# The gate by u moves into the first MLP, sums alternate between bank pairs, and weight decoding is spread over attention

## The chip, the cores and the metric

The kernel runs on one core of one Trainium2 chip. The metric is the device time in microseconds of one launch. The engines are TensorE (PE, with its weight loads as PEld), VectorE (DVE), ScalarE (ACT) and GpSimd (POOL). SyncE (SP) issues nearly all of the DMAs, in the order of the program.

## What is computed

Three stages follow one another, on 2 x 3008 = 6016 tokens of 256 features:

```python
scores = (1.0 / S) * np.matmul(z, z.transpose(0, 2, 1))     # z: 2 x 3008 x 64
x = u * np.matmul(np.maximum(scores, 0.0) ** 2, v)          # u, v: 2 x 3008 x 256
h = x @ w_in                                                # 256 x 2048
x = (s * np.maximum(h, 0.0) ** 2 + b) @ w_out               # 2048 x 256
h = x @ w_in2
out = (h / (1.0 + np.exp(-1.702 * h))) @ w_out2
```

The MLP weights come as 64-bit numbers. The kernel turns them into 32-bit ones with integer and float operations on DVE and ACT ("decoding").

## The kernel before

**Steps.** The work is a hand-written list of 288 attention steps and then 2 x 12 x 16 = 384 MLP steps. Each step has three parts: `up` (the first matmuls), `between` (what DVE and ACT do with their result) and `down` (matmuls that add into a sum). The main loop, at the end of the kernel, emits `up` and `between` four steps (`LAG`) ahead of `down`. Beside that, `when(step, f, ...)` hangs a piece of other work on a step: loads, splits, decoding. PE, DVE, ACT, POOL and the DMA queue of SP each run their instructions in the order in which this loop emits them.

**Attention.** Scores are symmetric, so each block of 512 x 512 is computed once. `Fresh` (a block of keys kc against a row of queries c) computes scores in `up`; in `between` it takes relu and square on ACT, turns the block in tiles of 32 on DVE (`turn`, when kc < c) and splits it into a high part (`hi`) and a rest (`lo`); in `down` it adds up six matmuls a step. The turned block is written to HBM (`park`, 1 MB) and read back later (`fetch`, 4 x 256 KB), and `Turned` uses it: `between` is only the split, `down` is six matmuls into a sum of its own, and at its end DVE adds that sum to x (line 384). A batch has rows c = 0 to 5, and row c has c + 1 fresh blocks of four steps each; a turned block runs between fresh ones, at least two blocks after its own. Batch 0 is steps 0 to 143, batch 1 steps 144 to 287. The last row of a batch (c = 5, 448 queries wide) is steps 96 to 143 and 240 to 287; it ends with two turned blocks in a row.

**Sums.** Each sum takes a pair of PSUM banks from `acc_pair`. `Fresh` always takes pair A, `Turned` always pair B, and the MLP alternates by token block. The next sum in a pair has to wait until the one before has been read: by the ACT copy of line 331 (a row's x) or by the DVE addition of line 384.

**The gate.** u is loaded transposed in tiles of 32 (`load_u`, line 170: four DMAs for half the features of one 512-token block, in runs of 128 bytes), turned on DVE (`turn_u`, line 182), and multiplied into x when the x of a block is complete. For c < 5 that is POOL at line 387, after the last addition; for c = 5 it is DVE at line 333, straight from the sum. The loads and turns hang on the steps around the end of each x, which lie at steps 106 to 140 and 250 to 284.

**Decoding.** `slots` gives the layer-0 weights the steps 20 to 179, one after the other, with five parts for each of 32 tiles: line 206, lines 209 and 211, line 215, line 218, line 224. The raw tile is loaded by line 193 or 195 six slots ahead, the result goes to HBM at line 227. Layer-1 weights are decoded in the same way during the first MLP. `fetch_w` (line 231) reads a decoded tile back five steps ahead of `split_w` (lines 237 and 238); for layer 0 that is steps 244 to 278.

**First MLP.** `split_x` makes a high part and a rest of x for a token block, 9 steps ahead of the block's first step (15 for block 0). A token block is 16 steps.

Of the kernel before, what the change touches and what calls it, by code (L numbers as in the profile page):

```python
# [11 lines left out]
ALU = mybir.AluOpType  # L12
# [3 lines left out]
def attention_mlp_mlp_kernel(  # L16
# [20 lines left out]
    nc = tc.nc  # L37
    B, S, D = u.shape
# [3 lines left out]
    P = 128  # L42
    CH = 512
    TPC = CH // P
# [31 lines left out]

    def mid_tile(name, dtype=F32):
        kind = name[0]
        bufs = {"z": 3, "w": 4, "u": 5}[kind]
        return mid.tile([P, CH], dtype, tag=kind, name=name, bufs=bufs)  # L80

    def acc_pair(which, name):
        return [acc_p.tile([P, CH], F32, tag=f"acc{which}", name=f"{name}{d}") for d in range(2)]

    def width(c):
        return min(CH, S - c * CH)

    zA, zB, vt, uT, xT = {}, {}, {}, {}, {}
    staged = {}

    def queries(bb, c):
# [67 lines left out]
        eng = nc.vector if (bb, c) == (0, 0) else nc.gpsimd  # L163
        eng.tensor_tensor(out=w[:, 1, :], in0=raw[:, t, :], in1=w[:, 0, :], op=ALU.subtract)  # L164

    def load_u(bb, c, h):
        n = width(c)
        ur = mid_tile(f"ur_{bb}_{c}_{h}").rearrange("p (t a) -> p t a", a=32)
        for i in range(4):
            nc.sync.dma_start(  # L170
                out=ur[32 * i : 32 * i + 32, : n // 32, :],
                in_=u[bb, c * CH : c * CH + n, h * P + 32 * i : h * P + 32 * i + 32].rearrange(
                    "(t b) a -> b t a", b=32
                ),
            )
        staged["u", bb, c, h] = ur

    def turn_u(bb, c, h):
        n = width(c)
        ur = staged.pop(("u", bb, c, h))  # L180
        uT[bb, c, h] = mid_tile(f"ut_{bb}_{c}_{h}")
        nc.vector.transpose(out=uT[bb, c, h][:, :n], in_=ur[:, : n // 32, :].rearrange("p t a -> p (t a)"))


    wi, wo = {}, {}
# [69 lines left out]
    class Fresh:  # L255
# [60 lines left out]

        def down(self):
            if (self.kc, self.t) == (0, 0):
                self.acc[:] = acc_pair("A", "acc")
            last = self.kc == self.c and self.t == TPC - 1  # L320
            add_up(
                self.acc, vt[self.bb, self.kc, self.t], self.hi, self.lo, self.n,
                (self.kc, self.t) == (0, 0), last, self.whole,
            )
            if not last:
                return
            bb, c, n = self.bb, self.c, self.n
            x = xT[bb * NCH + c] = big_tile(f"x_{bb}_{c}").rearrange("p (d n) -> p d n", d=2)
            for d in range(2):
                if c < LASTC:  # L330
                    nc.scalar.copy(out=x[:, d, :n], in_=self.acc[d][:, :n])  # L331
                else:
                    nc.vector.tensor_tensor(
                        out=x[:, d, :n], in0=self.acc[d][:, :n], in1=uT[bb, c, d][:, :n], op=ALU.mult
                    )

    def park(bb, kc, c):
        H = staged["H", bb, kc, c] = hbm.tile([P, 4 * CH], F32, tag=f"H_{bb}_{kc}_{c}", name=f"H_{bb}_{kc}_{c}")
# [9 lines left out]
    class Turned:  # L348
# [23 lines left out]

        def down(self):
            if self.t == 0:
                self.acc[:] = acc_pair("B", "tac")
            last = self.t == TPC - 1
            add_up(
                self.acc, vt[self.bb, self.c, self.t], self.hi, self.lo, CH, self.t == 0, last, self.whole
            )
            if not last:  # L380
                return
            x = xT[self.bb * NCH + self.kc]
            for d in range(2):
                nc.vector.tensor_tensor(out=x[:, d, :], in0=self.acc[d], in1=x[:, d, :], op=ALU.add)  # L384
            if self.c == LASTC:
                for d in range(2):
                    nc.gpsimd.tensor_tensor(
                        out=x[:, d, :], in0=x[:, d, :], in1=uT[self.bb, self.kc, d], op=ALU.mult
                    )

    def tokens(m):

        return m // NCH * S + m % NCH * CH, width(m % NCH)

    class Mlp:
        def __init__(self, layer, m, j, acc):
# [30 lines left out]
        def down(self):  # L427
            n, j = self.n, self.j
            w = wo[self.layer, j]
            if j == 0:  # L430
                self.acc[:] = acc_pair("AB"[self.m % 2], "accm")
            first, last = j == 0, j == NF - 1
            terms = ((0, self.hi), (1, self.hi), (0, self.lo))
            order = [(i, d) for i in range(3) for d in range(2)]
            if last:
                order.sort(key=lambda x: x[1])
            for i, d in order:
                h, g = terms[i]
                nc.tensor.matmul(  # L439
                    self.acc[d][:, :n],  # L440
                    w[:, h, d * P : (d + 1) * P],
                    g[:, :n],
                    start=first and i == 0,
                    stop=last and i == 2,
                )
            if last:
                self.post()
# [37 lines left out]
    steps, at = [], {}  # L485
    waiting, nblocks = [], 0

    def turned_blocks(least):
        while waiting and waiting[0][0] <= nblocks - least:
            _, bb, kc, c = waiting.pop(0)  # L490
            acc = []
            for t in range(TPC):
                at["t", bb, kc, c, t] = len(steps)
                steps.append(Turned(bb, kc, t, c, acc))
            if least:
                return

    for bb in range(B):
        for c in range(NCH):
            acc = []  # L500
            for kc in range(c + 1):
                for t in range(TPC):
                    at["f", bb, kc, c, t] = len(steps)
                    steps.append(Fresh(bb, kc, t, c, acc))
                nblocks += 1
                turned_blocks(APART)
                if kc < c:
                    waiting.append((nblocks, bb, kc, c))
        turned_blocks(0)
    for layer in range(2):  # L510
        for m in range(NM):
            acc = []
            for j in range(NF):
                at["m", layer, m, j] = len(steps)
                steps.append(Mlp(layer, m, j, acc))
# [4 lines left out]
    def when(step, f, *args):  # L520
        todo.setdefault(step, []).append((f, args))

    for bb in range(B):
        for c in range(NCH):
            first = at["f", bb, 0, c, 0]
            v0 = min(at["f", bb, c, c, 0], at.get(("t", bb, 0, c, 0), len(steps)))
            if (bb, c) == (0, 0):
                sz = -20
                when(-40, load_z, bb, c)
                when(-38, load_v, bb, c)  # L530
            else:
                sz = first - LAG - 8 if (bb, c) != (0, 1) else first - LAG - 4
                when(max(sz - 8, -39 if c < 2 else -LAG), load_z, bb, c)
                when(max(v0 - LAG - 12, -30), load_v, bb, c)
            for i in range(3):
                when(sz + i, split_z, bb, c, i)
            for t in range(TPC):
                when(v0 + t - LAG + 1, split_v, bb, c, t)
            for kc in range(c):
                when(at["f", bb, kc, c, TPC - 1] - LAG, park, bb, kc, c)  # L540
                when(at["t", bb, kc, c, 0] - LAG - 8, fetch, bb, kc, c)
            end = at["t", bb, c, LASTC, TPC - 1] if c < LASTC else at["f", bb, c, c, TPC - 1]
            for h in range(2):
                when(end - 9 + h, load_u, bb, c, h)
                when(end - 3 + h, turn_u, bb, c, h)
    ends = [at["f", B - 1, kc, LASTC, TPC - 1] + 1 for kc in range(LASTC)]
    slots = (range(20, ends[0] - 16), range(at["m", 0, 0, 10], len(steps)))
    for layer in range(2):
        n = 0
        for j in range(NF):  # L550
            for k in range(2):
                when(slots[layer][max(n - 6, 0)], load_w, layer, j, k)
                for part in range(5):
                    when(slots[layer][n], decode_w, layer, j, k, part)
                    n += 1
        for j in range(NF):
            if layer == 0:
                p = ends[min(j // 3, LASTC - 1)] + 2 * (j - 3 * min(j // 3, LASTC - 1))
            elif j < 2:
                p = at["m", 0, NM - 1, 0] - 12 + 6 * j  # L560
            else:
                p = at["m", 0, NM - 1, j - 1]
            when(p - 5, fetch_w, layer, j)
            when(p, split_w, layer, j)
    for layer in range(2):
        for m in range(NM):
            for k in range(2):
                when(at["m", layer, m, 0] - (9 if m else 15) + 2 * k, split_x, layer, m, k)

    warm = const.tile([P, 1], F32, name="warm")  # L570
    zeros = mid_tile("unused", mybir.dt.bfloat16)
# [57 lines left out]
```

## Time and profile before

| | us |
|---|---|
| median of 3 runs | 1565.5 (1565.25 to 1567.1) |
| the profiled execution's own time | 1567.48 |
| its span | 1565.7 |
| PE busy | 1514.9 (97% of the span) |
| DVE busy | 1122.8 (72%) |
| ACT busy | 906.7 (58%) |
| POOL busy | 68.5 (4%) |

Attention ends at about 540 us; the two MLPs fill the rest. The shares above are means over stages that differ, so the views that count are those by stretch. A stretch of steps is found on the time axis by its matmuls: step 104 begins its `down` at 193.45 us, step 144 at 276.31, step 160 at 311.52, step 252 at 462.77; the last matmuls of attention end at 539.35.

### The profile page before, as it was taken

The page shows a single profiled execution, that of the slowest core. Times are in us where ns is not written, and L with a number is a line of the kernel's source. Part 1 is how long each engine was busy: PE and PEld are TensorE (multiplying, and loading weights), DVE is VectorE, ACT ScalarE, POOL GpSimd, SP SyncE. Part 2 cuts the span into 40 slices and gives each one's busy share as a digit, 9 for nine tenths or more (in the row PEclk, how much of TensorE's full clock was granted, in tenths as well). Part 3 has the DMA queues.
Part 4 walks back from the last instruction along what each step waited for, and adds up shares of the span by engine and source line. Part 5 has one row for each costly group of instructions (what it writes and reads, how often), then busy time and mean ns, then how long its engine had stood idle before and what let it go on. Part 6 is the DMA issues. An engine that isn't in the chain of part 4 may idle for free.

```text
span 1565.7 us, 19611 instructions
## 1 busy us (share of the span) xinstructions
PE 1514.9 (97%) x6664; PEld 1252.9 (80%) x6664; DVE 1122.8 (72%) x2093; ACT 906.7 (58%) x1626; POOL 68.5 (4%) x69
## 2 busy tenths in 40 slices
PE   8999996899998799999999999999999999999998
PEld 5788874678886588888988888888888888888887
DVE  7799998887688867777777777785555555555554
ACT  7788763787886455555555555574444444444443
POOL 0100021200001200000000000000000000000000
PEclk9999997999999999999999999999999999999999
DMA  4587798456769401001010101120000000000001
GB/s 115 137 229 205 200 251 174 136 166 160 188 180 230 96 0 34 28 21 41 21 41 21 41 21 41 41 68 1 14 14 14 14 14 12 14 14 14 4 11 26
DMA packets 176197, 119.52 MB, mean 76 GB/s; under 512 B 130272, under 2 KB 144608, under 8 KB 172256
## 3 DMA queue, kind: packets, MB, share of 16 engines
q1 hardware_dynamic: 173184, 117.90, 29.8%
q8 instruction: 52, 0.85, 0.2%
q10 hardware_dynamic: 2912, 0.36, 0.1%
q14 instruction: 49, 0.40, 0.1%
HBM read 72.22 MB, written 46.01 MB: 76 GB/s over the span
## 4 chain that ended last, share of the span: by engine, by line
PE 86%; DMA 4%; DVE 4%; ACT 3%; issue 2%; SPq 1%; POOL 0%; DVEq 0%; ACTq 0%; POOLq 0%
PE accm L439 33%; PE ps_h L407 33%; PE acc L248 3%; PE acc L249 3%; PE acc L253 3%; PE tac L248 2%; PE tac L249 2%; PE tac L253 2%; DMA wb<-wfh 2%; PE ps_s L271 2%; PE ps_s L272 2%; DMA ur<-in_u_dram 1%; ACT a L278 1%; DMA R<-H 1%; ACT a L277 1%
## 5 line engine op out<-in xcount | busy, mean ns | idle before, releaser
L439 PE MATMUL accm<-hi,w 128*128 128x512 f32 (+1 forms) x1536 | 408.6, 385 | 0.0
L425 DVE TENSOR_TENSOR lo<-a,hi 128x512 fp32r<-128x512 f32 (+1 forms) x384 | 262.0, 682 | 150.0 <-ACT hi L424 130.0
L439 PEld LDWEIGHTS accm<-hi,w 128*128 128x128 f32 x1536 | 288.3, 188 | 53.7
L407 PE MATMUL ps_h<-Tx,w 128*128 128x512 f32 x1152 | 292.8, 389 | 0.0
L407 PE MATMUL ps_h<-Rx,w 128*128 128x512 f32 (+1 forms) x1152 | 283.0, 381 | 0.0
L407 PEld LDWEIGHTS ps_h<-Tx,w 128*128 128x128 f32 x1152 | 216.5, 188 | 44.6
L417 ACT ACTIVATE a<-ps_h 128x512 f32<-128x512 f32 (+1 forms) x192 | 113.3, 590 | 236.5 <-PE ps_h L407 236.2
L407 PEld LDWEIGHTS ps_h<-Rx,w 128*128 128x128 f32 x1152 | 216.3, 188 | 36.6
L439 PE MATMUL accm<-lo,w 128*128 128x512 f32 (+1 forms) x768 | 237.3, 385 | 0.0
L424 ACT CAST hi<-a 128x512 fp32r<-128x512 f32 (+1 forms) x192 | 117.4, 611 | 149.4 <-DVE a L423 149.4
L423 DVE TENSOR_TENSOR a<-ps_h,a 128x512 f32<-128x512 f32 (+1 forms) x192 | 130.3, 679 | 93.9 <-ACT a L422 92.7
L422 ACT ACTIVATE a<-ps_h 128x512 f32<-128x512 f32 (+1 forms) x192 | 113.3, 590 | 119.9 <-PE ps_h L407 119.6
L419 DVE TENSOR_SCALAR a<-a,sb 128x512 f32<-128x512 f32 (+1 forms) x192 | 105.0, 547 | 88.2 <-ACT a L418 87.8
L439 PEld LDWEIGHTS accm<-lo,w 128*128 128x128 f32 x768 | 144.1, 188 | 27.0
L248 PE MATMUL acc<-hi,v 128*128 128x512 f32 (+1 forms) x336 | 132.1, 393 | 15.0 <-ACT x L331 6.3
L249 PE MATMUL acc<-hi,v 128*128 128x512 f32 (+1 forms) x336 | 130.7, 389 | 1.7 <-POOL v L164 1.7
L418 ACT ACTIVATE a<-a 128x512 f32<-128x512 f32 (+1 forms) x192 | 119.6, 623 | 6.1
L289 DVE TENSOR_TENSOR lo<-a,hi 128x512 fp32r<-128x512 f32 (+1 forms) x166 | 115.9, 698 | 3.7
L277 ACT ACTIVATE a<-ps_s 128x512 f32<-128x512 f32 (+1 forms) x168 | 97.1, 578 | 32.3 <-PE ps_s L272 32.1
L248 PE MATMUL tac<-hi,v 128*128 128x512 f32 x240 | 97.5, 406 | 16.2 <-DVE x L384 13.2
L278 ACT ACTIVATE a<-a 128x512 f32<-128x512 f32 (+1 forms) x168 | 103.7, 617 | 5.3
L253 PE MATMUL acc<-lo,v 128*128 128x512 f32 (+1 forms) x332 | 102.0, 389 | 0.0
(66 smaller groups left out, 1617.4 us busy)
## 6 DMA issues: line engine op xcount, KB each, us to landing
H<-T SPq DMA_DIRECT2D x30, 1024.0 KB, 5.0
R<-H SPq DMA_DIRECT2D x120, 256.0 KB, 6.4
wr<-in_moe_w_in_dram SPq DMA_DIRECT2D x32, 256.0 KB, 2.8
wr<-in_moe_w_out_dram SPq DMA_DIRECT2D x32, 256.0 KB, 2.8
wfh<-wf SPq DMA_DIRECT2D x32, 256.0 KB, 2.0
wb<-wfh SPq DMA_DIRECT2D x32, 256.0 KB, 3.6
vr<-in_v_dram SPq DMA_DIRECT2D x40, 128.0 KB, 4.8
ur<-in_u_dram SPq DMA_DIRECT2D x80, 64.0 KB, 2.7
```

The lines of the kernel that those rows point to most:

```text
L248: nc.tensor.matmul(acc[d][:, :n], w[:, 0, cols], hi, start=first, stop=False)
L249: nc.tensor.matmul(acc[d][:, :n], w[:, 1, cols], hi, start=False, stop=last and not whole)
L253: nc.tensor.matmul(acc[d][:, :n], w[:, 0, cols], lo, start=False, stop=last)
L278: nc.scalar.activation(out=a[:, :n], in_=a[:, :n], func=AF.Square)
L289: nc.vector.tensor_tensor(out=lo[:, :n], in0=a[:, :n], in1=hi[:, :n], op=ALU.subtract)
L407: nc.tensor.matmul(self.p[:, :n], w[:, h, k, :], x[:, k, :n], start=i == 0, stop=i == len(terms) - 1)
L417: nc.scalar.activation(out=a[:, :n], in_=self.p[:, :n], func=AF.Relu)
L418: nc.scalar.activation(out=a[:, :n], in_=a[:, :n], func=AF.Square)
L423: nc.vector.tensor_tensor(out=a[:, :n], in0=self.p[:, :n], in1=a[:, :n], op=ALU.mult)
L424: nc.scalar.copy(out=hi[:, :n], in_=a[:, :n])
L425: nc.vector.tensor_tensor(out=lo[:, :n], in0=a[:, :n], in1=hi[:, :n], op=ALU.subtract)
L439: nc.tensor.matmul(self.acc[d][:, :n], w[:, h, d * P : (d + 1) * P], g[:, :n], start=first and i == 0, stop=last and i == 2,)
```

## The change

1. `Fresh` and `Turned` no longer take fixed pairs of banks. `other_set()` hands out A and B in turn as the list of steps is built, so a sum never follows another one directly in the same pair.
2. x is not gated in attention. Lines 333 and 387 go; the x of c = 5 is copied by ACT like the others. A new `gate` turns u on DVE and multiplies it into x on POOL. It hangs 16 steps ahead of each token block's first step in the first MLP (24 for block 0), `load_u` 26 steps ahead (48 for block 0).
3. The layer-0 decoding takes 160 slots spread evenly over steps 20 to 226.
4. `fetch_w` runs 8 steps ahead of `split_w` (5 before). The tiles of kind `w` have 5 buffers (4 before), those of kind `u` 4 (5 before).

```diff
-        bufs = {"z": 3, "w": 4, "u": 5}[kind]
+        bufs = {"z": 3, "w": 5, "u": 4}[kind]
...
-    def turn_u(bb, c, h):
-        n = width(c)
-        ur = staged.pop(("u", bb, c, h))
-        uT[bb, c, h] = mid_tile(f"ut_{bb}_{c}_{h}")
-        nc.vector.transpose(out=uT[bb, c, h][:, :n], in_=ur[:, : n // 32, :].rearrange("p t a -> p (t a)"))
+    def gate(m, h):
+        n = tokens(m)[1]
+        ur = staged.pop(("u", m, h))
+        ut = mid_tile(f"ut_{m}_{h}")
+        nc.vector.transpose(out=ut[:, :n], in_=ur[:, : n // 32, :].rearrange("p t a -> p (t a)"))
+        x = xT[m][:, h, :n]
+        nc.gpsimd.tensor_tensor(out=x, in0=x, in1=ut[:, :n], op=ALU.mult)
...
             for d in range(2):
-                if c < LASTC:
-                    nc.scalar.copy(out=x[:, d, :n], in_=self.acc[d][:, :n])
-                else:
-                    nc.vector.tensor_tensor(
-                        out=x[:, d, :n], in0=self.acc[d][:, :n], in1=uT[bb, c, d][:, :n], op=ALU.mult
-                    )
+                nc.scalar.copy(out=x[:, d, :n], in_=self.acc[d][:, :n])
...
-                self.acc[:] = acc_pair("B", "tac")
+                self.acc[:] = acc_pair(self.acc.pop(), "tac")
...
-            if self.c == LASTC:
-                for d in range(2):
-                    nc.gpsimd.tensor_tensor(
-                        out=x[:, d, :], in0=x[:, d, :], in1=uT[self.bb, self.kc, d], op=ALU.mult
-                    )
...
+    last_set = ["B"]
+
+    def other_set():
+        last_set[0] = "AB"[last_set[0] == "A"]
+        return last_set[0]
...
-            acc = []
+            acc = [other_set()]
+            mine = acc[0]
             for kc in range(c + 1):
+                last_set[0] = mine
...
-            end = at["t", bb, c, LASTC, TPC - 1] if c < LASTC else at["f", bb, c, c, TPC - 1]
-            for h in range(2):
-                when(end - 9 + h, load_u, bb, c, h)
-                when(end - 3 + h, turn_u, bb, c, h)
...
-    slots = (range(20, ends[0] - 16), range(at["m", 0, 0, 10], len(steps)))
+    turns = range(20, ends[0] - 16)
+    slots = ([turns[i * len(turns) // (10 * NF)] for i in range(10 * NF)], range(at["m", 0, 0, 10], len(steps)))
...
-            when(p - 5, fetch_w, layer, j)
+            when(p - 8, fetch_w, layer, j)
...
+                if layer == 0:
+                    when(at["m", layer, m, 0] - (26 if m else 48) + k, load_u, m, k)
+                    when(at["m", layer, m, 0] - (16 if m else 24) + 2 * k, gate, m, k)
```

## Rows read from the trace of the kernel before

**Rows 1.** The page's 40 equal slices of the span, in tenths.

```profile
PE   8999996899998799999999999999999999999998
DVE  7799998887688867777777777785555555555554
PEclk9999997999999999999999999999999999999999
DMA  4587798456769401001010101120000000000001
```

**Rows 2.** Busy time by stretch: us, engines with instruction counts, granted clock, DMA share, GB/s.

```profile
181.06:193.45 12.39, 12.39 (x59) 10.89 (x58) 12.22 (x35) 10.93 (x21) 0.00 (x0) 1.00 0.75 227
193.45:276.31 82.86, 65.91 (x269) 50.80 (x268) 75.53 (x159) 46.29 (x91) 17.05 (x14) 0.90 0.89 207
276.31:311.52 35.21, 30.17 (x121) 23.31 (x120) 29.94 (x54) 26.82 (x51) 7.71 (x8) 0.95 0.51 142
444.30:462.77 18.47, 18.47 (x89) 16.53 (x88) 15.93 (x43) 15.43 (x33) 0.00 (x0) 1.00 0.89 248
462.77:539.35 76.58, 61.96 (x254) 47.71 (x253) 65.58 (x128) 44.94 (x96) 15.59 (x12) 0.96 0.84 190
...
540.00:1050.00 510.00, 510.00 (x2291) 429.61 (x2290) 383.06 (x787) 275.20 (x489) 2.73 (x2) 1.00 0.10 32
```

**Rows 3.** DVE groups by line, 193.45 to 276.31: busy us, mean ns, idle before.

```profile
L367 DVE TENSOR_TENSOR lo<-R,hi 128x512 fp32r<-128x512 f32 x15 | 12.9, 863 | 0.0
L182 DVE STREAM_TRANSPOSE ut<-ur 128x512 f32<-128x512 f32 (+1 forms) x12 | 8.3, 693 | 1.2 <-POOL x L387 1.2
...
L224 DVE SCALAR_TENSOR_TENSOR wf<-fr,pw 128x256 f32<-128x256 f32 x8 | 4.9, 617 | 0.1
...
L218 DVE SCALAR_TENSOR_TENSOR pw<-wr,pw 128x256 uint32<-128x256 uint32 x8 | 3.8, 476 | 0.0
L215 DVE SCALAR_TENSOR_TENSOR fr<-wr,mt 128x256 f32<-128x256 uint32 x9 | 3.7, 410 | 0.0
...
L211 DVE TENSOR_SCALAR mt<-wr 128x256 uint32<-128x256 uint32 x8 | 3.3, 410 | 0.1
L206 DVE TENSOR_SCALAR pw<-wr 128x256 uint32<-128x256 uint32 x8 | 2.2, 276 | 3.1 <-DMA wr<-in_moe_w_out_dram 2.6 <-DMA wr<-in_moe_w_in_dram 0.5
...
L333 DVE TENSOR_TENSOR x<-acc,ut 128x448 f32<-128x448 f32 x2 | 1.1, 616 | 0.0
```

**Rows 4.** The same view, 340 to 430 us, where POOL does little.

```profile
L367 DVE TENSOR_TENSOR lo<-R,hi 128x512 fp32r<-128x512 f32 x24 | 15.5, 685 | 2.3 <-ACT hi L364 2.3
...
L224 DVE SCALAR_TENSOR_TENSOR wf<-fr,pw 128x256 f32<-128x256 f32 x2 | 0.8, 418 | 0.0
```

**Rows 5.** POOL groups by line, 193.45 to 276.31.

```profile
L387 POOL TENSOR_TENSOR x<-x,ut 128x512 f32<-128x512 f32 x8 | 11.7, 1482 | 46.9 <-DVE x L384 46.9
L164 POOL TENSOR_TENSOR v<-vr,v 128x256 fp32r<-128x256 f32 x6 | 5.4, 909 | 59.7 <-ACT v L162 59.7
```

**Rows 6.** Timeline of SP's queue: start, us, DMAs issued.

```profile
514.40 11.81 SPq L170 DMA_DIRECT2D ur<-in_u_dram  x16
```

**Rows 7.** DVE and ACT groups, 462.77 to 528.62.

```profile
L238 DVE TENSOR_TENSOR w<-wb,w 128x256 fp32r<-128x256 f32 x26 | 13.0, 539 | 4.2 <-ACT w L237 4.1
...
L182 DVE STREAM_TRANSPOSE ut<-ur 128x512 f32<-128x512 f32 (+1 forms) x10 | 6.9, 690 | 1.2 <-POOL x L387 1.2
...
L237 ACT CAST w<-wb 128x256 fp32r<-128x256 f32 x26 | 9.2, 403 | 20.3 <-DMA wb<-wfh 20.3
```

**Rows 8.** What PE waited for, 200 to 330 us: total, times, longest.

```profile
PE tac L248 <- DVE x L384: 9.7, 1, 9.7
PE tac L253 <- DVE lo L367: 4.6, 5, 1.7
PE acc L248 <- ACT x L331: 4.3, 2, 3.0
```

**Rows 9.** The same view, 0 to 200 us.

```profile
PE acc L248 <- ACT x L331: 1.9, 2, 1.3
```

**Rows 10.** Busy time of one token block (16 steps) of the first MLP.

```profile
544.79:587.50 42.71, 42.71 (x190) 35.34 (x190) 30.61 (x59) 21.76 (x37) 0.26 (x1) 1.00 0.00 0
```

More of the change, by code (lines that the diff above doesn't have):

```diff
@@ L86, in width, with tokens @@
         return min(CH, S - c * CH)
-    zA, zB, vt, uT, xT = {}, {}, {}, {}, {}
+    def tokens(m):
+        return m // NCH * S + m % NCH * CH, width(m % NCH)
+    u_rows = u.rearrange("b s d -> (b s) d")
+    zA, zB, vt, xT = {}, {}, {}, {}
     staged = {}
@@ L164, in split_v, with load_u @@
         eng.tensor_tensor(out=w[:, 1, :], in0=raw[:, t, :], in1=w[:, 0, :], op=ALU.subtract)
-    def load_u(bb, c, h):
-        n = width(c)
-        ur = mid_tile(f"ur_{bb}_{c}_{h}").rearrange("p (t a) -> p t a", a=32)
+    def load_u(m, h):
+        start, n = tokens(m)
+        ur = mid_tile(f"ur_{m}_{h}").rearrange("p (t a) -> p t a", a=32)
         for i in range(4):
@@ L171, in load_u @@
                 out=ur[32 * i : 32 * i + 32, : n // 32, :],
-                in_=u[bb, c * CH : c * CH + n, h * P + 32 * i : h * P + 32 * i + 32].rearrange(
+                in_=u_rows[start : start + n, h * P + 32 * i : h * P + 32 * i + 32].rearrange(
                     "(t b) a -> b t a", b=32
@@ L175, in load_u @@
             )
-        staged["u", bb, c, h] = ur
-    def turn_u(bb, c, h):
-        n = width(c)
-        ur = staged.pop(("u", bb, c, h))
-        uT[bb, c, h] = mid_tile(f"ut_{bb}_{c}_{h}")
-        nc.vector.transpose(out=uT[bb, c, h][:, :n], in_=ur[:, : n // 32, :].rearrange("p t a -> p (t a)"))
+        staged["u", m, h] = ur
+    def gate(m, h):
[5 more added lines that the diff above has]
+        nc.gpsimd.tensor_tensor(out=x, in0=x, in1=ut[:, :n], op=ALU.mult)
     wi, wo = {}, {}
@@ L318, in down @@
             if (self.kc, self.t) == (0, 0):
-                self.acc[:] = acc_pair("A", "acc")
+                self.acc[:] = acc_pair(self.acc.pop(), "acc")
             last = self.kc == self.c and self.t == TPC - 1
@@ L384, in down @@
                 nc.vector.tensor_tensor(out=x[:, d, :], in0=self.acc[d], in1=x[:, d, :], op=ALU.add)
-            if self.c == LASTC:
-                for d in range(2):
-                    nc.gpsimd.tensor_tensor(
-                        out=x[:, d, :], in0=x[:, d, :], in1=uT[self.bb, self.kc, d], op=ALU.mult
-                    )
-    def tokens(m):
-        return m // NCH * S + m % NCH * CH, width(m % NCH)
     class Mlp:
@@ L430, in down @@
             if j == 0:
-                self.acc[:] = acc_pair("AB"[self.m % 2], "accm")
+                self.acc[:] = acc_pair(self.acc.pop(), "accm")
             first, last = j == 0, j == NF - 1
@@ L499, in attention_mlp_mlp_kernel @@
         for c in range(NCH):
-            acc = []
+            acc = [other_set()]
+            mine = acc[0]
             for kc in range(c + 1):
+                last_set[0] = mine
                 for t in range(TPC):
@@ L511, in attention_mlp_mlp_kernel @@
         for m in range(NM):
-            acc = []
+            acc = [other_set()]
             for j in range(NF):
```

## The prediction

> **What bounds the kernel now.** I read the slices first, then a table by stretch, then the groups and waits of the stretches that stand out. The slices show PE full from slice 15 to the end, so the MLPs are bound by matmuls, and show PE dipping around slices 6, 7 and 12 to 14, with DVE and the DMA engines high just there [rows 1]. These dips are the ends of the two batches, where the last row's steps, the gate and the start of something new come together. From about 540 to 1050 us PE is busy all 510.00 us [rows 2]: nothing done to the first MLP can make it shorter, only longer.
>
> How much can be won? In a clean stretch of the last row 59 matmuls take 12.39 us, 0.210 us each; in that of batch 1, 89 take 18.47, 0.2075 [rows 2]. **Tail 0** (steps 104 to 143, 193.45 to 276.31 us) has 269 matmuls; at 0.210 they need 56.5 us, the stretch takes 82.86, so 26.4 are lost. The **boundary** (steps 144 to 159) has 121 wide matmuls; at 0.229 (one of 0.2267 in a full MLP stretch, 42.71 us for 190 and some partial ones [rows 10], and a little over) they need 27.7 of 35.21, so 7.5 are lost. **Tail 1** (steps 252 to 287) has 254; at 0.215, between the narrow pace and the wide one, they need 54.6 of 76.58, so 22.0 are lost. That is 56 us, and PE can win no more than this there.
>
> What holds PE back in the tails? In tail 0 DVE is busy 75.53 of 82.86 us (91%) and the DMA share is 0.89; in tail 1 65.58 of 76.58 (86%) and 0.84 [rows 2]. PE's largest waits near tail 0 are for DVE: 9.7 us for the addition of line 384, 4.6 for `lo` [rows 8]. The 9.7 is named as a bank wait (the second of two turned blocks needs pair B), but the addition is late because DVE has 75 us of work against 56.5 of PE's. So DVE bounds tail 0. In tail 1 DVE is high too, and ACT, in order, stands 20.3 us waiting for weights read back (line 237), with `hi` and relu queued behind it [rows 7]; these reads are late because the DMA engines and SP's queue are full of u. The clock follows: it averages 0.90 in tail 0 and 0.96 in tail 1, against 1.00 in the full stretches [rows 2], after PE has stood idle.
>
> **The change, part by part.**
>
> *Tail 0, DVE.* The 12 turns of u go: 8.3 us by their durations [rows 3]. Durations on DVE overlap a little (the groups of the stretch sum to more than its busy time), so I take 0.63 each, 7.6. The two products from PSUM go, 1.1 [rows 3]; as copies on ACT they last about as long, on an engine busy 46.29 of 82.86 [rows 2]. Decoding is 4.9 + 3.8 + 3.7 + 3.3 + 2.2 = 17.9 us in the five groups [rows 3]; 160 slots over 207 steps instead of 160 leave 0.77 of it, so 4.1 go, some 3.7 after overlap. The eight POOL products go, 11.7 of POOL's 17.05 us [rows 2, 5]. They cost DVE too: `lo` of line 367 averages 863 ns here against 685 where POOL does little, line 224 617 against 418 [rows 3, 4]. That is 15 x 0.178 = 2.7 and 8 x 0.2 = 1.6 in these two groups, and by the same proportion about 7 over all; two thirds of it (11.7 of 17.05), say 4.9, go with the products. DVE's 75.53 becomes 75.53 - 7.6 - 1.1 - 3.7 - 4.9 = 58.2, against PE's 56.5: the two would be even.
>
> *Tail 0, DMA and SP.* Sixteen loads of u that ran alone took SP 11.81 us, 0.74 each [rows 6]. Tail 0 has 48, so 35 us of the 74 in which the DMA engines were busy (0.89 x 82.86) go, and the queue of SP is free for `park` and `fetch`. DMA stops being near full.
>
> With DVE and PE even, neither can lag and catch up. DVE now reaches 91% of the stretch; at 91% 58.2 us of work take 64. **Term: 82.9 - 64 = 19.** Its bounds are 9 (only the two u groups and what POOL cost, half of it lost again to the next latency) and 26 (all of PE's loss).
>
> *Boundary.* PE waits 4.3 us in two waits for the ACT copy of line 331, because rows 0, 1 and 2 of a batch follow one another in pair A [rows 8]; with alternating pairs the next sum starts in the other one. **Term: 4**, bounds 0 (the same latency shows up as a wait for `hi`) and 7.5. At the start of batch 0 the same waits are 1.9 us [rows 9]. **Term: 1.9**, bounds 0 and 1.9. What alternating gives between the turned blocks (the 9.7) is in tail 0's term already, since that wait is DVE's lag.
>
> *Tail 1.* Twelve turns of u at 0.63 go and the two of block 0 come (its gate hangs on steps 264 and 266): 6.3 less. The products from PSUM give 1.1. POOL was busy 15.59 us [rows 2], three quarters of it products; its cost on DVE, seen in line 238 at 539 ns [rows 7], falls by about 4.3, with block 0's two products counted back. DVE goes from 65.58 to 53.9, PE needs 54.6, ACT has about 46. The wait of 20.3 us for weights loses its cause twice: 40 of 48 loads of u are gone (30 us of DMA; block 0's eight are at step 240 and block 1's eight at step 278, after the last weight), and the reads start three steps earlier with one buffer more. What is late next is DVE, as in tail 0. At 89%, a little better than now because the ACT waits go, 53.9 us take 60.5. **Term: 76.6 - 60.5 = 16**, bounds 8 and 22.
>
> *Decoding in batch 1.* Steps 180 to 226 now carry decoding. Batch 0 ran the same rows with decoding at full density; from 181.06, with DVE busy 12.22 of 12.39 us, PE lost nothing [rows 2]. At 0.77 of that density the cost is nothing; bound 2. If the cover failed, each step would add about a third of a microsecond of DVE.
>
> *First MLP.* Each token block gets two turns (2 x 0.69 us, [rows 3]) and two POOL products (2 x 1.48, [rows 5]). DVE is busy 30.61 of 42.71 us in a block [rows 10], so 12.1 are idle; the turns and, at worst, DVE standing still for the products take 4.4. The gate is emitted 7 steps (19 us) ahead of `split_x`, and u 10 steps (27 us) ahead of the gate; eight issues at 0.74 and the queue's lag fit. I take 0; if the cover were gone the cost would be 12 x 4.4 = 52. Behind a late turn stand `hi` and `lo` of the next steps on DVE, and PE waits for those four steps later.
>
> One row and one rule differ. Line 367 grows by 26% while POOL is busy a fifth of the stretch [rows 3 to 5], so POOL slows DVE by a part of its own time, 7 of 17 us. The Trainium skill ("SBUF — State Buffer", section "SBUF: two separate sides") says that the port pair which DVE and GpSimd share is an exclusive lock: an operation with two SBUF inputs or the GpSimd one holds it "for the whole instruction" and the other fully blocks. By that rule moving 11.7 us of products would free 11.7 of DVE in tail 0, not 4.9, and the forecast would be some 7 us lower up to PE's own bound; it is also the rule that speaks against the gate in the first MLP, where it gives the 4.4 us per block that I compared with 12.1.
>
> **Sum.** 19 + 4 + 1.9 + 16 = 41 us off the profiled execution's 1567.5, 1526.5. The median of the runs is 2.0 below that execution, so **1524.5**.
>
> **The rivals.**
>
> *The tails come down to PE's own need.* If moved products free more of DVE than I count, and with no idle the clock stays full, the gains are 26.4 + 6 + 1.9 + 22 - 1 = 55: 1510. For it: DVE would have slack. Against: even then the last two turned blocks have little other work beside them.
>
> *The tails stay bound by the round trip.* A turned block is written (`park`), read back, split and used within a few steps, with two buffers on each side; if that chain, not DVE's load, sets the pace of the last blocks, each tail keeps about 9 us more than I count: 41 - 18 = 23, so 1542.5. For it: DMA shares of 0.84 to 0.89. Against: PE's large waits there name DVE's work and line 331, none of them the read back block [rows 8].
>
> *Slower.* DVE in the first MLP turns u late: its transpose stands in order before `hi` and `lo`, and if u's DMA waits on SP behind a decoded tile's write, DVE stands still with everything behind it. It decides from the point where a block costs more than 41 / 12 = 3.4 us of PE; at the uncovered 4.4 per block the sum is +52 - 41 = +11: 1576.5. Against: 27 us of lead and 12 idle us per block.
>
> **How the numbers follow.** Forecast 0.55, PE's need 0.15, round trip 0.23, slower 0.05, and 0.02 that gains and costs cancel. The range runs from 1509 (all of PE's need met) to 1543 (the round trip), leaving out less than 2 in 10. Faster by over 0.2% (3 us, about what a measurement of this kernel can tell from no change) has 0.93, the same 0.02, slower 0.05.
>
> **What would show it.** After: attention ends near 500 us instead of 539; tail 0 is 62 to 66 us with DVE still the busiest beside PE, DMA share near 0.6 in it; no wait of PE for line 331; no long wait of ACT for weights; PE full in the first MLP, with DVE near 33 of 42.7 us a block. I am wrong if PE shows gaps at the token blocks of the first MLP, if tail 0 stays above 72 us, or if steps 180 to 226 stretch.

## The result and the profile after

The changed kernel takes 1519.1 us (median of 4 runs, 1518.45 to 1519.45) against 1566.3 for the kernel before beside it: a ratio of 0.970 (95% interval 0.968 to 0.972), 47 us less. The forecast was 1524.5 in 1509 to 1543. Its profiled execution has a span of 1517.3 us, 48.4 less than before.

The slices of the page, with the 40 equal slices in tenths (the lines that answer to [rows 1]):

```profile
PE   8999999999999999999999999999999999999998
DVE  7799899989899788887878888765555555555554
PEclk9999999999999999999999999999999999999999
DMA  4587776866696112103021210200000000000001
```

The dips of PE around slices 6, 7 and 12 to 14 are gone. The load of DVE is spread more evenly over attention and is higher in the first MLP; DMA has small peaks in the first MLP, where u is now loaded.

Busy time by stretch of the kernel after, the columns as in [rows 2]: steps 104 to 135, 136 to 143, the boundary, steps 252 to 286, and two token blocks of the first MLP.

```profile
190.32:235.46 45.14, 45.14 (x215) 40.20 (x214) 42.29 (x104) 34.86 (x68) 3.70 (x4) 1.00 0.83 219
235.46:250.57 15.11, 13.49 (x56) 9.63 (x54) 13.02 (x25) 8.93 (x18) 0.53 (x1) 1.00 0.92 198
250.57:282.94 32.37, 30.32 (x121) 21.91 (x122) 30.12 (x52) 27.41 (x52) 7.04 (x8) 1.00 0.45 129
433.94:489.88 55.94, 54.50 (x250) 45.82 (x248) 52.61 (x116) 44.77 (x96) 6.51 (x6) 1.00 0.79 212
497.80:540.50 42.70, 42.70 (x190) 35.36 (x189) 32.01 (x59) 22.46 (x38) 2.26 (x3) 1.00 0.14 31
540.50:583.20 42.70, 42.70 (x190) 35.37 (x189) 34.27 (x68) 22.81 (x39) 2.23 (x2) 1.00 0.19 50
```

Tail 0, the first two lines together, takes 60.25 us for 82.86 before [rows 2]; DVE is busy 55.31 of them, 92%, and PE 58.63, 97%. PE is idle 1.6 us of the second line, 2.1 of the boundary and 1.4 of steps 252 to 286, and its granted clock is 1.00 in all. The two MLP lines show the price of the gate in its new place: DVE 32 to 34 us of 42.7 (30.6 before [rows 10]), POOL two, PE not a microsecond. From the start of step 287 to the end of the span both kernels take 1027.4 us.

Not all of the 48.4 us is idle time. The same 6664 matmuls keep PE busy 1499.2 us after, 1514.9 before, so 15.7 us are matmuls that run faster: the granted clock in tail 0 was 0.90 and is 1.00.

What PE waited for from 200 to 330 us, after (it answers to [rows 8]; totals, times, longest):

```profile
PE tac L256 <- DVE hi L374: 1.2, 2, 0.9
PE acc L257 <- POOL v L170: 1.1, 2, 0.6
PE acc L256 <- ACT v L168: 0.7, 1, 0.7
PE acc L256 <- DVE hi L292: 0.6, 1, 0.6
PE acc L256 <- ACT a L285: 0.4, 1, 0.4
PE acc L261 <- DVE lo L297: 0.2, 1, 0.2
```

No wait names the addition (line 384, now 387) or the copy of x (331, now 338). What is left is small: 4.2 us, of which 1.8 are for the splits of batch 1's first values (lines 168 and 170).

### The profile page after: what moved, and what is told of

Same layout as the page of the kernel before. It is cut to its first block, busy times and chain, and to the rows that moved or that the text cites. A ratio compares the mean times of both kernels' runs of the same rounds, so it can differ in the third digit from the quotient of the medians.

```text
span 1517.3 us, 19598 instructions
## 1 busy us (share of the span) xinstructions
PE 1499.2 (99%) x6664; PEld 1248.9 (82%) x6664; DVE 1127.4 (74%) x2089; ACT 906.1 (60%) x1630; POOL 75.2 (5%) x73
## 4 chain that ended last, share of the span: by engine, by line
PE 92%; DMA 2%; DVE 2%; ACT 1%; SPq 1%; issue 1%; DVEq 0%; ACTq 0%
PE ps_h L401 34%; PE accm L433 34%; PE acc L256 4%; PE acc L261 4%; PE acc L257 4%; PE tac L257 3%; PE tac L256 3%; PE tac L261 3%; PE ps_s L279 2%; PE ps_s L280 2%; DMA vr<-in_v_dram 1%; DMA R<-H 1%; DMA wr<-in_moe_w_in_dram 0%; SPq L152 0%; DVE lo L297 0%
## 5 line engine op out<-in xcount | busy, mean ns | idle before, releaser
L414 DVE CAST hi<-a 128x512 fp32r<-128x512 f32 (+1 forms) x192 | 96.0, 500 | 20.0 <-DVE a L413 0.5
```

## Where the time went: one table

The start of each step's first `down` matmul, read from PE's timeline, cuts attention into stretches. Steps 16 to 103 (146.3 to 146.5 us) and 160 to 251 (150.6 to 151.4) are the same in every kernel below, also where they now carry decoding. The rest, in us (the last column ends where step 287 begins), with the time of the whole as a ratio to the kernel before, its 95% interval and the median:

| kernel | 0-15 | 104-135 | 136-143 | 144-159 | 252-279 | 280-286 | ratio | median us |
|---|---|---|---|---|---|---|---|---|
| before | 32.5 | 51.6 | 31.3 | 35.2 | 51.0 | 24.5 | 1 | 1566 to 1567 |
| after | 29.3 | 45.1 | 15.1 | 32.4 | 41.0 | 14.9 | 0.970 (0.968 to 0.972) | 1519.1 |
| **before, one part alone** | | | | | | | | |
| banks | 29.3 | 52.2 | 24.2 | 37.0 | 51.0 | 19.4 | 0.991 (0.990 to 0.993) | 1554.0 |
| decode | 32.1 | 49.6 | 33.0 | 32.1 | 50.7 | 25.8 | 0.997 (0.996 to 0.998) | 1562.2 |
| gate | 31.8 | 49.7 | 22.3 | 34.6 | 50.9 | 16.5 | 0.987 (0.985 to 0.988) | 1546.7 |
| early | 31.8 | 51.5 | 30.9 | 37.1 | 46.4 | 25.4 | 0.998 (0.997 to 0.999) | 1563.4 |
| **after, one part undone** | | | | | | | | |
| a_fixed | 32.6 | 45.2 | 23.6 | 33.4 | 41.0 | 16.7 | 0.977 (0.975 to 0.979) | 1532.2 |
| a_dense | 29.6 | 48.8 | 15.3 | 33.8 | 41.0 | 15.0 | 0.973 (0.971 to 0.974) | 1524.9 |
| a_late | 29.4 | 45.2 | 15.2 | 32.4 | 48.7 | 16.3 | 0.975 (0.973 to 0.977) | 1527.7 |
| a_gate | 29.5 | 49.6 | 26.5 | 36.9 | 46.5 | 18.3 | 0.987 (0.985 to 0.988) | 1546.2 |
| **after, one cost put back** | | | | | | | | |
| a_dma | 29.7 | 46.7 | 21.3 | 32.3 | 47.6 | 17.8 | 0.980 (0.978 to 0.982) | 1535.9 |
| a_dve | 29.9 | 46.0 | 17.7 | 32.5 | 44.2 | 16.0 | 0.974 (0.973 to 0.976) | 1526.6 |
| a_pool | 29.7 | 46.8 | 16.1 | 35.0 | 44.6 | 16.8 | 0.976 (0.975 to 0.978) | 1529.7 |
| **after, changed further** | | | | | | | | |
| soon | 30.0 | 45.7 | 14.6 | 32.3 | 39.2 | 15.6 | 0.969 (0.967 to 0.970) | 1518.0 |

The parts alone save 13.2 + 5.0 + 20.5 + 3.1 = 42 us by the medians; undone singly they cost 13.1 + 5.7 + 27.1 + 8.5 = 54; together they save 47. So they help one another, most of all in steps 252 to 279.

## The experiments

### The bank pairs

*banks*: the kernel before, with this part of the diff alone.

```diff
-                self.acc[:] = acc_pair("B", "tac")
+                self.acc[:] = acc_pair(self.acc.pop(), "tac")
...
-            acc = []
+            acc = [other_set()]
+            mine = acc[0]
```

> The kernel before with the alternating bank pairs alone; gate, decoding and fetches stay. Theory (VectorE's load bounds the batch ends, the 9.7 us bank wait is VectorE's lag): only the boundary and the start of each batch gain, 4 + 3 us, ratio near 0.995, and the first tail (steps 104 to 143) stays above 78 us. Rival (the bank waits themselves are the cost): 9.7 + 4.3 + 3.1 + 1.9 = 19 us, ratio 0.988, first tail near 73 us.

*a_fixed*: the kernel after with pairs A and B as before.

```diff
-                self.acc[:] = acc_pair(self.acc.pop(), "acc")
+                self.acc[:] = acc_pair("A", "acc")
...
-                self.acc[:] = acc_pair(self.acc.pop(), "tac")
+                self.acc[:] = acc_pair("B", "tac")
```

> The kernel after with fixed pairs again (A for fresh rows, B for turned blocks). Theory: the boundary and the starts lose 4 + 3 us and the last two turned blocks of each batch about 1 each, so 6 to 9 us above the kernel after, ratio to before near 0.975. Rival (bank waits are a cost of their own): 19 us above it, ratio 0.982.

Measured: 13.2 us less alone, 13.1 more when undone. That is about midway between the two forecasts, and so is the first tail of *banks*, 76.4 us (theory above 78, rival 73). Of the 14 us of span in a_fixed, 8.5 lie in steps 136 to 143, 3.3 in steps 0 to 15, 1.8 at the end and 1.0 at the boundary. The prediction had put the wait between turned blocks down to DVE's load, but in a_fixed the gate is gone, DVE is busy only 59.44 of 68.79 us in tail 0, and the wait is there. PE's timeline of a_fixed at the second of the two turned blocks (start, us, and in brackets the idle time and what ended it):

```profile
252.55 0.77 PE L256 MATMUL tac<-hi,v 128*128 128x512 f32 x1 [7.24 <-DVE x L387]
253.11 0.63 PE L257 MATMUL tac<-hi,v 128*128 128x512 f32 x1
```

And DVE's timeline in the same kernel, while PE stood still from 245.3 to 252.5:

```profile
246.44 0.71 DVE L130 STREAM_TRANSPOSE zt<-zr 128x512 f32<-128x512 f32 x1 [1.79 <-DMA zr<-in_z_dram]
247.08 0.65 DVE L370 TENSOR_TENSOR lo<-R,hi 128x512 fp32r<-128x512 f32 x1
...
249.14 0.69 DVE L370 TENSOR_TENSOR lo<-R,hi 128x512 fp32r<-128x512 f32 x1
249.75 0.68 DVE L145 TENSOR_TENSOR zb<-zt,za 64x512 fp32r<-64x512 f32 x1
250.35 0.28 DVE L219 TENSOR_SCALAR mt<-wr 128x256 uint32<-128x256 uint32 x1
250.66 0.69 DVE L374 TENSOR_TENSOR hi<-R,hi 64x512 fp32r<-64x512 f32 x1
251.38 0.42 DVE L223 SCALAR_TENSOR_TENSOR fr<-wr,mt 128x256 f32<-128x256 uint32 x1
251.72 1.28 DVE L387 TENSOR_TENSOR x<-tac,x 128x512 f32<-128x512 f32 x2
```

The addition that frees the pair stands last in this list. DVE takes its instructions in order, and the loop has emitted ahead of the addition the splits of the four steps to come, the keys of batch 1 and the decoding; the first of them waits 1.79 us for a load. With one pair, PE must wait for all of that; with the other pair free it goes on, as the splits it needs are among the work done first. The kernel after shows this: DVE runs the same list in the same order, with the addition at 248.81, and PE works through that time. PE's clock drops in the wait as well: the 14 matmuls from 252.55 to 258.62 start 0.43 us apart, the next ones 0.23, and the granted clock of steps 136 to 143 is 0.78, as against 1.00 after. At 0.23 the 14 would have taken 3.3 us instead of 6.1, so the wait costs about 2.8 us more than its 7.2. The part is a decoupling: it is worth what DVE's queue holds in front of the addition, not only DVE's overload.

### The decoding

*decode*: the kernel before with the spread slots alone. *a_dense*: the kernel after with the slots as before.

```diff
-    slots = ([turns[i * len(turns) // (10 * NF)] for i in range(10 * NF)], range(at["m", 0, 0, 10], len(steps)))
+    slots = (turns, range(at["m", 0, 0, 10], len(steps)))
```

> The kernel before with the decoding spread over steps 20 to 226 alone. Theory (VectorE bounds the first tail): 3.7 us less work there at 91% busy, so 4 us less, ratio 0.997; the second tail unchanged. Rival (transfers bound both tails): the weight loads are 9 of some 100 transfers of the first tail, so at most 1 us.

> The kernel after with the decoding in steps 20 to 179 again, one part per step. Theory (VectorE and the transfers of the first end are both near full): 4 to 6 us above the kernel after, in steps 104 to 159. Rival (with the gate gone there is room): under 2 us.

The sizes are as forecast, 5.0 us less alone and 5.7 more when undone; the place is so only for the second. Undone, 3.7 lie in steps 104 to 135, where DVE and the DMA engines are near full, and 1.4 at the boundary. Alone, the first tail gives 0.2 and not 4: steps 104 to 135 give 1.9, which steps 136 to 143 with their bank wait (12.7 us there) take back, and 3.1 come at the boundary. The later steps that carry the decoding instead (180 to 226) take no longer in any kernel.

### The gate

*gate*: the kernel before with the gate moved alone. *a_gate*: the kernel after with the gate back in attention (its loads, turns and products at their old steps, a fifth u buffer).

> The kernel before with the gate moved into the first MLP alone (fixed pairs, dense decoding, fetches five steps ahead, buffers as before). Theory: VectorE in the first tail 75.5 - 7.6 - 1.1 - 4.9 = 62 us at 91%, so 68 instead of 83; second tail 61 to 64 instead of 76.6; together 28 us, ratio 0.982. Rival (PE's own need is reached as soon as the gate is gone): 26 + 20 us, ratio 0.971. If the bank waits were the cost: the 9.7 us would stay, first tail near 74.

> The kernel after with the gate by u back in attention (loads, turns and products where the kernel before has them; alternating pairs, spread decoding and early fetches stay). The three pieces put back singly cost 17.7, 8.4 and 10.3 us of span. If they use resources in turn (each lengthens the same chain), 33 to 38 us above the kernel after; if they run beside one another, the largest decides: 18 to 24 us.

Alone it saves 20.5 us, less than the 28 expected: 9.0 in steps 136 to 143, 8.0 in 280 to 286, 1.8 in 104 to 135, and **0.1 in steps 252 to 279**, where I had expected most of tail 1's gain. The first tail takes 72.1 us, between the 68 of the theory and the 74 if the bank wait stayed: PE still waits 5.7 us there for the addition. Undone, it costs 27.1 us, 28.7 by the spans.

### Which of the gate's costs it was

Three kernels put one cost each back into the kernel after, at the old steps. *a_dma* loads u there a second time, into tiles nobody reads (it and *a_dve* have a fifth u buffer for them):

```diff
+                when(end - 9 + h, idle_load, bb * NCH + c, h)
```

> The kernel after with the loads of u issued a second time, at the steps where the kernel before had them, into tiles that nobody reads (five buffers of that kind). Theory (VectorE bounds the ends): transfers alone cost 0 to 3 us in both ends. Rival (DMA engines and SyncE's queue bind): 48 x 0.74 = 35 us more transfer time at each end, so the first end near 75 us instead of 60 and the second near 68 instead of 57; 20 us or more in all.

*a_dve* makes 24 turns of tiles of x there, into tiles nobody reads:

```diff
+        nc.vector.transpose(out=out[:, :n], in_=xT[bb * NCH + min(c, LASTC - 1)][:, h, :n])
...
+                when(end - 3 + h, idle_turn, bb, c, h)
```

> The kernel after with 24 extra transposes on VectorE, where the kernel before turned u, from tiles of x into tiles that nobody reads. Theory: VectorE in the first end 55.3 + 7.6 = 63 us, at 92% 68 instead of 60; in the second 54 + 7.6 = 62, so 66 instead of 57; 12 to 17 us in all. Rival (transfers or PE bind, VectorE has room): under 4 us.

*a_pool* multiplies x by ones on POOL there:

```diff
+            if self.c == LASTC:
+                for d in range(2):
+                    nc.gpsimd.tensor_tensor(out=x[:, d, :], in0=x[:, d, :], in1=ones, op=ALU.mult)
```

> The kernel after with 20 extra products on GpSimd, x times a tile of ones, where the kernel before multiplied by u. Theory (GpSimd costs VectorE about 0.4 of its own time): 4.9 us of VectorE at each end, 2 to 6 us in each. By an exclusive lock: 11.7 us of VectorE at each end, 9 to 13 us in each. Rival (VectorE has room): under 2 us in all.

By the spans: loads 17.7 us (the rival said 20 or more), turns 8.4 (between the 12 of the theory and the 4 of the rival), products 10.3 (2.6 in tail 0 and 5.5 in steps 252 to 286, as the theory's 2 to 6; the lock's 9 to 13 did not come). My theory that DVE alone bounds the tails falls: the transfers, for which it allowed 3 us, are the largest piece. They sum to 36.4, and the whole gate put back costs 28.7. By place: in steps 104 to 159 the pieces cost 16.5 singly and 20.4 together: there they add up. In steps 252 to 286 they cost 19.2 singly and 8.9 together, less than the 9.5 of the loads alone (a_dma keeps the new loads of u besides): there they overlap.

How do the loads cost that much? SP's queue is full: in steps 252 to 286 of a_dma one DMA follows another, and four loads of u, 64 KB each in runs of 128 bytes, hold the queue as long as four reads of 256 KB. Timeline of SP's queue in a_dma, the last reads of turned blocks in attention (start, us, DMAs):

```profile
476.46 3.63 SPq L188 DMA_DIRECT2D ul<-in_u_dram  x4
480.20 3.32 SPq L360 DMA_DIRECT2D R<-H  x4
483.62 0.38 SPq L250 DMA_DIRECT2D wb<-wfh  x1
484.04 2.00 SPq L188 DMA_DIRECT2D ul<-in_u_dram  x4
486.46 2.32 SPq L250 DMA_DIRECT2D wb<-wfh  x1
488.83 2.04 SPq L188 DMA_DIRECT2D ul<-in_u_dram  x4
490.97 1.85 SPq L360 DMA_DIRECT2D R<-H  x4
```

The last read, that of the block of steps 284 to 287, is issued 48.8 us after step 252 began (442.18). In the kernel after it is 33.6 us (467.58, with step 252 at 433.94):

```profile
462.48 2.93 SPq L349 DMA_DIRECT2D R<-H  x4
465.51 0.91 SPq L239 DMA_DIRECT2D wb<-wfh  x2
467.58 2.36 SPq L349 DMA_DIRECT2D R<-H  x4
470.80 9.24 SPq L176 DMA_DIRECT2D ur<-in_u_dram  x8
```

So ACT stands waiting for the read block. Its largest wait in steps 252 to 286 of a_dma, and of the kernel after:

```profile
ACT hi L378 <- DMA R<-H: 14.1, 3, 5.6
```

```profile
ACT hi L367 <- DMA R<-H: 3.2, 2, 2.4
```

In tail 0 of a_dma it is the same: the last read is issued 49.4 us after step 104 began, 38.8 in the kernel after, and ACT waits 12.4 us for read blocks, 2.7 in the kernel after. This is the round trip that the prediction had as a rival. It bounds the kernel after once the loads of u stand in its queue; it was not yet the bound before. There ACT waits 1.6 us for the read block in tail 0, where DVE is 91% busy, and in steps 252 to 286 no wait of ACT names it; there ACT waits 20.3 us for weights. What these three runs price is a cost in the kernel after, not a share of the 48 us.

The turns: in a_dve DVE is busy 5.1 us more in steps 104 to 143 (44.28 + 16.12 against 42.29 + 13.02) for the 10 turns that lie there, and 6.5 more in steps 252 to 286 for 12. That is 0.51 and 0.54 us each, where I took 0.63.

The products: DVE in steps 252 to 286, first in a_pool, then in the kernel after (busy us, mean ns).

```profile
L246 DVE TENSOR_TENSOR w<-wb,w 128x256 fp32r<-128x256 f32 x26 | 14.0, 583 | 0.0
L370 DVE TENSOR_TENSOR lo<-R,hi 128x512 fp32r<-128x512 f32 x15 | 12.5, 862 | 0.0
L297 DVE TENSOR_TENSOR lo<-a,hi 128x448 fp32r<-128x448 f32 x14 | 9.5, 679 | 0.1
L315 DVE STREAM_TRANSPOSE T<-a 128x384 f32<-128x384 f32 x10 | 5.7, 566 | 0.6 <-ACT a L286 0.5
L387 DVE TENSOR_TENSOR x<-tac,x 128x512 f32<-128x512 f32 x8 | 5.1, 681 | 0.0
...
L417 DVE CAST hi<-a 128x512 fp32r<-128x512 f32 x3 | 2.3, 751 | 0.2
L416 DVE TENSOR_SCALAR a<-a,sb 128x512 f32<-128x512 f32 x3 | 2.2, 739 | 0.4 <-ACT a L415 0.4
```

```profile
L246 DVE TENSOR_TENSOR w<-wb,w 128x256 fp32r<-128x256 f32 x26 | 10.8, 460 | 0.0
L370 DVE TENSOR_TENSOR lo<-R,hi 128x512 fp32r<-128x512 f32 x15 | 10.3, 721 | 0.3 <-ACT hi L367 0.3
L297 DVE TENSOR_TENSOR lo<-a,hi 128x448 fp32r<-128x448 f32 x14 | 9.6, 682 | 0.1
L315 DVE STREAM_TRANSPOSE T<-a 128x384 f32<-128x384 f32 x10 | 5.7, 566 | 0.6 <-ACT a L286 0.5
L387 DVE TENSOR_TENSOR x<-tac,x 128x512 f32<-128x512 f32 x8 | 5.1, 682 | 0.0
...
L413 DVE TENSOR_SCALAR a<-a,sb 128x512 f32<-128x512 f32 x3 | 1.6, 544 | 1.7 <-ACT a L412 1.7
```

POOL is busy 11.7 us more (18.19 against 6.51), DVE 7.0 more (59.60 against 52.61): 0.6 of POOL's time, where the prediction took 0.42; in tail 0 it is 5.3 for 10.2. The means hide how it comes about. POOL and DVE of a_pool around two of the products:

```profile
455.40 3.00 POOL L390 TENSOR_TENSOR x<-x,ones 128x512 f32<-128x512 f32 x2 [7.38 <-DVE x L387]
455.84 1.41 DVE L370 TENSOR_TENSOR lo<-R,hi 128x512 fp32r<-128x512 f32 x1
457.17 1.84 DVE L246 TENSOR_TENSOR w<-wb,w 128x256 fp32r<-128x256 f32 x2
```

A subtraction of line 370 mostly lasts 0.68 us in this stretch, here 1.41; of the two of line 246 one lasts its usual 0.42, the first 1.51. Each starts while a product runs and ends 0.3 to 0.6 us after it. In this stretch eight products lengthen eight instructions: three of line 370 (by 0.73 each), three of 246 (by 1.09), the cast of 417 (by 0.97) and the tensor-scalar of 416 (by 0.59). These sum to the 7.0 us. The group of line 297 subtracts SBUF tiles too and stays as it was, 682 and 679, since none of these eight products lengthens one of it. The turn, and the addition that reads one operand from PSUM, do not grow, the addition not even where it runs beside the start of a product. So a product costs DVE not a share of its time but one instruction's wait. A part of a_pool's cost is another one: at the boundary PE waits 5.3 us for the split of v, since POOL works in order and a product waits there for its addition.

```profile
PE acc L257 <- POOL v L170: 5.3, 2, 3.6
```

### The fetches of decoded weights

*a_late*: the kernel after with five steps of lead and the buffers as before. *early*: the kernel before with eight steps and a fifth buffer alone.

```diff
-        bufs = {"z": 3, "w": 5, "u": 4}[kind]
+        bufs = {"z": 3, "w": 4, "u": 5}[kind]
...
-            when(p - 8, fetch_w, layer, j)
+            when(p - 5, fetch_w, layer, j)
```

> The kernel after with the decoded weights fetched five steps ahead again, four buffers for them and five for u. Theory (ScalarE's waits for weights end by the earlier fetch and the fifth buffer): the steps 252 to 279 go from 41 back to 51 us, 10 us above the kernel after. Rival (the prediction's step: they end because the loads of u are gone): at most 2 us above it.

> The kernel before with the decoded weights fetched eight steps ahead and five buffers for them alone; everything else stays. Theory after the runs so far (the ScalarE waits for weights are a matter of lead): they fall below 5 us and the steps 252 to 279 take about 46 us instead of 51, so 5 to 7 us less. Rival (the loads of u delay the weights whatever the lead): no change.

a_late costs 8.5 us, 7.7 of them in steps 252 to 279, where the theory said 10, and ACT's wait for weights is back, though the loads of u are gone:

```profile
ACT w L245 <- DMA wb<-wfh: 14.3, 8, 3.6
```

So in this stretch the lead and the fifth buffer end the wait, not the missing loads. No run tells these two apart, but SP's queue points to the lead: from 434 to 475 us of a_late it stands still 25.0 us at the write of a turned block (line 342), until DVE has turned its last part, with the weights' reads behind it in order, and only 1.5 us for a buffer of theirs. In early the long waits for weights are gone too, and steps 252 to 279 fall by 4.6 us; over all it gives 3.1, not the 5 to 7 forecast. The 4.6 is less than the 7.7: ACT now waits for the turned block's read, 4.9 us, and once 5.5 more at the same line until a load of u has landed. In a_gate, with the fetches early and the gate in its old place, that wait is 16.6 us.

```profile
ACT hi L364 <- DMA R<-H: 16.6, 4, 6.3
```

That explains the zero of *gate* alone: with the old lead, ACT waits for the weights whether u is loaded there (20.3 us) or not (14.6). With the old lead the stretch takes 49 to 51 us, with the gate in its old place and the new lead 46.4 and 46.5; only with both changed is it 41, also where one of the other two parts is undone (a_fixed, a_dense).

### A further step

*soon*: the kernel after with the first loads of batch 1's z and v earlier, and the first gate out of tail 1.

```diff
-                when(max(sz - 8, -39 if c < 2 else -LAG), load_z, bb, c)
-                when(max(v0 - LAG - 12, -30), load_v, bb, c)
+                when(max(sz - (20 if bb and c < 2 else 8), -39 if c < 2 else -LAG), load_z, bb, c)
+                when(max(v0 - LAG - (24 if bb and c < 2 else 12), -30), load_v, bb, c)
...
-                    when(at["m", layer, m, 0] - (26 if m else 48) + k, load_u, m, k)
-                    when(at["m", layer, m, 0] - (16 if m else 24) + 2 * k, gate, m, k)
+                    when(at["m", layer, m, 0] - (26 if m else 72) + k, load_u, m, k)
+                    when(at["m", layer, m, 0] - (16 if m else 56) + 2 * k, gate, m, k)
```

> The kernel after with the loads of z and v for batch 1's first two blocks 12 steps earlier, and block 0's gate 32 steps earlier, out of the second end. In the kernel after, the chain through steps 136 to 159 runs over these loads. Theory: 2 to 4 us below the kernel after. Rival (they only collide with the turned blocks' reads, which have the same queue): the same or up to 3 us slower.

0.969 (0.967 to 0.970) beside 0.970 (0.968 to 0.972): the two cannot be told apart, so the 2 to 4 us forecast are not there. By the profile steps 252 to 279 fall by 1.8 us, where the first gate had been, and 136 to 143 by 0.5, and other stretches give 2.0 back (0.7 in 0 to 15, 0.6 in 104 to 135, 0.7 in 280 to 286). The boundary does not move (32.3 and 32.4), so the steps of these loads were not what holds it.

## Why the prediction was right, and where it was not

- **Sign and size.** 48.4 us of span went, 41 were forecast. The work in the MLP costs nothing, as forecast: 12 idle microseconds of DVE per token block took it up. So the slower rival falls. 48.4 lies midway between the forecast and the rival "PE's own need" (55). In the tails that rival is what came, and I gave it too little: PE is idle 1.6 us in tail 0 and 1.4 in tail 1. Its 55 was too high because PE's need was set too low: tail 0 keeps PE busy 58.6 us at full clock, not 56.5 (the pace of the 448 wide stretch was used for the 512 wide turned blocks too), and the boundary 30.3, not 27.7. That the sum came within 7 us is in part luck: terms had the wrong cause, as follows.
- **Tail 0** gave 22.6, forecast 19. DVE's remaining work was 55.3 us, forecast 58.2. It reaches 92%, forecast 91%, but that agreement is luck: PE, busy 97%, sets the 60.25 us, not DVE "at 91%". DVE's load was a real cause before, but too narrow a one. "DMA stops being near full" failed: the share is 0.85, forecast near 0.6. The step took 35 us of SP's queue time off the 74 us that the DMA engines were busy; they are busy 51 us now (0.85 x 60.25), so some 22 went. And the sum priced the transfers at nothing beside DVE: put back alone into the kernel after, the loads cost 7.8 us in tail 0, more than the turns (3.5) and the products (2.6) together, by way of SP's queue and the read of turned blocks. The round trip was set aside because PE's waits did not name the read block; in a_dma it is ACT that waits for it, and PE for ACT.
- **The banks in tail 0.** "That wait is DVE's lag" and so "in tail 0's term already" failed. With the gate gone the fixed pair still costs 8.5 us in steps 136 to 143. The two errors met in one term: what I gave to DVE's load was partly the banks'. The clock had no term of its own: matmuls that run faster are 7.3 of tail 0's 22.6 us (PE busy 65.91 before, 58.63 after) and 6.4 of tail 1's 19.6.
- **The start and the boundary.** 3.2 us at the start, forecast 1.9. It is the pair's (3.3 in both of its runs); what it cost beside the listed waits is not traced. The boundary gave 2.8, forecast 4; of these the pair is only 1.0 by a_fixed, spread decoding 1.4 by a_dense.
- **Tail 1** gave 19.6 (steps 252 to the last matmul: 76.6 to 57.0), forecast 16. The step that failed is its cause. The weights' reads were not late because "the DMA engines and SP's queue are full of u": with u's loads gone and the old lead ACT still waits 14.3 and 14.6 of the 20.3 us for them (a_late, gate), with u's loads and the new lead no long wait is left (early). "Loses its cause twice" should have been: two waits of ACT, one behind the other, one for weights with too little lead, one for read blocks behind u. Moving the gate alone gave nothing in steps 252 to 279, early fetches alone 4.6, both (with the rest) 10.
- **Decoding in batch 1** cost nothing, as forecast.
- **POOL and DVE.** The row-based 0.4 of POOL's time was low (0.5 in tail 0 and 0.6 in tail 1 by a_pool), one for one was too high. The Trainium skill ("SBUF — State Buffer", section "Who interferes with whom") also says that a DVE instruction with at most one SBUF input, outside the modes that use both ports, does not contend with GpSimd. The rows of a_pool agree as far as they go: single subtractions of two SBUF tiles grew, the turn and the addition from PSUM did not. A cast and a tensor-scalar grew too; whether these ran in such a mode no row here shows. The lock itself fits what a_pool shows, one instruction that waits out one product. The prediction used it for all of DVE's work and left the exception out.

What stays open: what the fifth buffer adds to the lead, and what holds the boundary at 32.4 us, 4.7 above its 27.7; only 2.1 of these are idle time of PE.

## What to carry to other kernels

When a wait on a PSUM bank names an engine that is busy, look at what stands in that engine's queue ahead of the instruction that frees the bank: a second pair of banks may be worth more than relieving the engine. Where several transfers share one queue, taking away one of them may show nothing until the next one in line has its lead too, so test the parts alone and undone; here 42 us alone and 54 undone bracket the 47 together. And before calling one engine the bound of a stretch in which another resource is as busy (here DVE 91% and the DMA engines 89%), put each cost back by itself, and read the result as a price in that kernel.

## What the runs showed of the hardware

Loads of u, 64 KB each in runs of 128 bytes, are dear on SP's queue: 16 took 11.81 us [rows 6], 0.74 each, and in a_dma four took 2.00 to 3.63 us where four reads of 256 KB took 1.85 to 3.32. Put back at the batch ends they delayed the last read of a turned block by 15 us.

A GpSimd product of 1.48 us in a_pool made one DVE instruction last longer and no more: a two-operand SBUF subtraction 1.4 us instead of 0.68, or 1.5 instead of 0.42, a cast 1.40 instead of 0.43, a tensor-scalar 1.13 instead of 0.54. The turn (566 ns) and the addition from PSUM (681 to 682) did not change.

After 7.24 us without a matmul, 14 matmuls of a_fixed started 0.43 us apart and the next ones 0.23.
